# Attention, a dense layer and experts on one core: the dense layer's first activation queued inside attention, the sum of v taken from a column of constants, the embeddings on GpSimd

## The chip, the cores and the metric

The kernel runs on one core of one Trainium2 chip. The metric is the device time of one execution in microseconds (us); the time shown for a kernel is the median of its runs.

## The reference

Three parts follow each other. The sizes are 2 batches, 8 heads, 768 tokens of 64 values for attention, 1536 tokens of 512 values for the layers behind it, 2048 hidden values in the dense layer, and 8 experts of 1024.

```python
mask = q_bucket[:, :, :, None] == k_bucket[:, :, None, :]      # 6 sign bits of q @ proj, k @ proj
scores = np.where(mask, scale * np.matmul(q, k.transpose(0, 1, 3, 2)), -1e9)
attn = np.exp(scores - np.max(scores, axis=-1, keepdims=True))
attn = attn / (np.sum(attn, axis=-1, keepdims=True) + 1e-09)
x = np.matmul(attn, v)                                         # then to [1536, 512]
h = x @ w_in
x = (h * np.tanh(softplus(h))) @ w_out                         # dense layer
logits = normalized(x) @ normalized(expert_emb).T / tau        # each token goes to its best expert
out = gate * (np.maximum(x @ w1[e], 0.0) @ w2[e])              # e, gate: of that expert
```

## The kernel before, in words

**Attention** (class `Attn`). Heads are taken one after the other, each in six key tiles of 128 keys. `run_all` (L473) is a loop over steps g from -2 to 101. A step computes the scores of one key tile (`score_unit`, L360: four matmuls into PSUM, and one Exp on ScalarE into an SBUF tile p of 128 keys x 768 queries), one and a half max units for a head further on (`max_unit`, L316, reduced by VectorE at L328 and L332), and two products with v for the key tile three steps back (`pv`, L395: each is two instructions, since the operands are 32 bits wide). p tiles come from a pool of five buffers. Everything else has a place in the table `AT` (L37), in sixths of a step counted from the head's first: `out0` and `out1` copy the two halves of a finished head out of PSUM (ScalarE, L425, and L427 for the sums of an odd head), `s_row` to `xlo` divide by the sums and split the result into two halves of 16 bits.

The sum of v, times 1e-9/768, is added to the product before the division. `v_red` (L374) adds the tiles of v on GpSimd in six instructions a pair of heads, `v_sum` (L384) sums over the 128 partitions with a small matmul (two instructions), `v_col` (L390) copies the column from PSUM with ScalarE, and `scale` (L455) adds it. They are placed at 2 to 17, at 62 and at 66 sixths of a step, in every second head: eight times in all.

**PSUM in attention** has eight banks: two score tiles of two banks each (`ps_s`), two buffers of the pool `ps_m` and two of `ps_o` for the products. `ps_m` serves the max tiles, the column sp of v_sum, the row transposes tm (L348, first heads only), the embedding's transposes tpe (L752), and the first two hidden tiles of the dense layer.

**The hook** (L1283) runs after every step. It takes one step of `emb` (L723: the experts' embeddings are normalized, split and transposed; the three instructions L744 to L746 run after step 8 and the transposes after step 10), computes the hidden tile of block 0 after step 95 and of block 1 after step 99 (`UP`), and takes one step of `w1_work` (L671), which splits the dense weights: three VectorE instructions (L700, L702, L682), then two on ScalarE (L709, L710) and a subtraction on GpSimd (L711). Two steps of it are left at the end of attention; the last tile goes through L716 (ScalarE) and L718 (VectorE).

**The dense layer** (`moe1`, L775) has 48 blocks G of 128 hidden values x 512 tokens. The hidden tile h of a block is 12 matmuls (`up`, L760), its product with w_out another 12 (L815), three blocks later. The activation between them is, on ScalarE, Tanh (L834), Square (L839), Square (L845), Exp (L848) and, behind VectorE's L857, Square (L861); then, in the next block's turn, VectorE's L836 and L841, ScalarE's conversion L850 and GpSimd's subtraction L851. Block 0 has PE compute the hidden tiles 2 to 5; from block 3 on each block computes one more, three ahead. A hidden tile's buffer is free after L841. The activation has four tiles t, w, u and p with two buffers each; L857 writes p from w and u, and L841 writes p again.

**Order.** `in_order` (L126) ties each engine's instructions to the order in which the program issues them, so an engine's queue is the order of the code. The experts (`moe2`) follow.

Of the kernel before, what the change touches and what calls it, by code (L numbers as in the profile page):

```python
# [20 lines left out]
P = 128  # L21
# [6 lines left out]
PB = 5  # L28
# [5 lines left out]
TEND = 101  # L34
RPB, CVB = 1, 3
STEP = 7
AT = dict(rows_t=-7, rows_in=-7, m_row=-22, bits=-102, max_end=-24, hi=-184, lo0=-156, lo1=-150, dup=-138, out_x=-147, in_x=-127, out_m=-99, in_m=-79, args=-103, load_kq=-210, load_v=-37, v_red=2, v_sum=62, v_col=66, out0=50, out1=54, s_row=55, inv=77, r_out=79, r_in=91, scale=112, xhi=127, xlo=139)  # L37
GAP = dict(bits=1, max_end=1, inv=1, v_red=3)
STEPS = dict(v_red=6, bits=3, max_end=2, inv=2)
FROM = dict(rows_in=1, m_row=4, bits=3, max_end=1, hi=4, lo0=4, lo1=4, dup=4, out_x=4, in_x=4, out_m=4, in_m=4, rows_t=1, args=3, load_kq=6, load_v=2)  # L40
UNTIL = dict(rows_t=4, rows_in=4)
EVERY = dict(load_kq=(2, 0), load_v=(2, 0), v_red=(2, 0), v_sum=(2, 0), v_col=(2, 0)) | {k: (2, 1) for k in ("inv", "r_out", "r_in", "scale", "xhi", "xlo")}
# [95 lines left out]
class Attn:  # L138
    def __init__(self, tc, ctx, q, k, v, proj, ident, ones, xx, dt, rest):
# [40 lines left out]
        self.tiny = cp.tile([P, 1], F32, name="tiny")  # L180
        nc.gpsimd.memset(self.tiny, 1e-9 / S)
# [14 lines left out]
    def warm(self, n, w=None):  # L196

        if w is None:
            w = self.ps_o.tile([P, HS], F32, tag="o", name="warmed")
        for _ in range(n):  # L200
            self.nc.tensor.matmul(w, self.ones, self.ones[:, 0:1].to_broadcast([P, HS]), start=True, stop=True)
# [158 lines left out]
    def score_unit(self, b, h, t):  # L360
        nc = self.nc
        z = self.Z[b, h]
        kq, m = z["x"], z["m"]
        ts = self.tok(b, h, t)
        s = self.ps_s.tile([P, 2, 512], F32, tag="s", name=f"s_{b}_{h}_{t}")[:, :, 0:HS]
        for c in range(2):
            nc.tensor.matmul(s[:, c, :], kq[:, 0, ts], kq[:, 1, c * HS : (c + 1) * HS], start=True, stop=False)  # L367
        for c in range(2):
            nc.tensor.matmul(s[:, c, :], m[0:97, 0, ts], m[0:97, 1, c * HS : (c + 1) * HS], start=False, stop=True)  # L369
        p = self.pp.tile([P, S], F32, tag="p", name=f"p_{b}_{h}_{t}", bufs=PB)  # L370
        nc.scalar.activation(p.rearrange("p (c n) -> p c n", c=2), s, AF.Exp, scale=2.0**-11)  # L371
        z["p"].append(p)

    def v_red(self, b, h):  # L374
        add = partial(self.nc.gpsimd.tensor_tensor, op=ALU.add)
        vs = self.Z[b, h]["vs"] = self.sm.tile([P, 2, D], F32, tag="vs", name=f"vs_{b}_{h}", bufs=1)
        for i in range(2):
            v = self.vn(b, h + i)
            t = self.sm.tile([P, 3, D], F32, tag="vt", name=f"vt_{b}_{h + i}", bufs=1)
            yield add(t, v[:, 0:3], v[:, 3:6])  # L380
            yield add(t[:, 0], t[:, 0], t[:, 1])
            yield add(vs[:, i], t[:, 0], t[:, 2])

    def v_sum(self, b, h):  # L384

        z = self.Z[b, h]
        z["sp"] = self.ps_m.tile([P, 1], F32, tag="m", name=f"sp_{b}_{h}")
        self.nc.tensor.matmul(z["sp"], z.pop("vs").rearrange("p i d -> p (i d)"), self.tiny, start=True, stop=True)

    def v_col(self, b, h):  # L390
        z = self.Z[b, h]
        z["col"] = self.sm.tile([P, 1], F32, tag="col", name=f"col_{b}_{h}")
        self.nc.scalar.copy(z["col"], z.pop("sp"))

    def pv(self, b, h, t, c):  # L395

        nc = self.nc
        z = self.Z[b, h]
        i, cs = h % 2, slice(c * HS, (c + 1) * HS)
        m = P if i else 65  # L400
        if t == 0:
            z["o", c] = self.ps_o.tile([P, HS], F32, tag="o", name=f"o_{b}_{h}_{c}")
        o = z["o", c][0:m, :]
        nc.tensor.matmul(o, self.vn(b, h, t), z["p"][t][:, cs], start=(t == 0), stop=(t == NJ - 1))  # L404

    def wide(self, b, h, tag, bufs):

        last = b == B - 1 and h >= H - 2
        name = tag
        pool, tag, bufs = (self.rest_pools[0], "stg", None) if last else (self.ou, tag, bufs)  # L410
        return pool.tile([P, S], F32, tag=tag, name=f"{name}_{b}_{h}", bufs=bufs)

    def out(self, b, h, c):

        z = self.Z[b, h]
        i, cs = h % 2, slice(c * HS, (c + 1) * HS)
        o = z.pop(("o", c))
# [32 lines left out]
    def r_in(self, b, h):  # L450
        self.rb = self.wide(b, h, "rb", 1)
# [154 lines left out]
class Moe:  # L606
# [116 lines left out]
    def emb(self, tp, ps):  # L723
# [50 lines left out]

    def moe1(self, side, more):  # L775
# [22 lines left out]
        for G in range(N + GLAG):  # L798
            c, F = divmod(G, NF1)
            if G < N:  # L800
                t, w, u, p = m[G] = [T(tag, G) for tag in "twup"]
# [36 lines left out]
            if G < N:  # L838
                nc.scalar.activation(w, t, AF.Square, scale=-0.5, bias=self.bias[0.5])  # L839
# [14 lines left out]
            for x in new[:NC]:  # L854
                x(0)
            if G < N:
                nc.vector.scalar_tensor_tensor(p, w, 1.0, u, op0=ALU.add, op1=ALU.mult)  # L857
# [3 lines left out]
                nc.scalar.activation(t, p, AF.Square, bias=self.bias[-1.5])  # L861
# [395 lines left out]
def moe_attn(ctx, tc, a):  # L1257
# [9 lines left out]
    with ExitStack() as c1:  # L1267
# [7 lines left out]
        with ExitStack() as c2, tc.using_default_side("right"):  # L1275
# [88 lines left out]
```

## Time and profile before

| | |
|---|---|
| runs | 704.41 us median of 3 (703.2 to 705.53) |
| profiled execution | 708.11 us, of it a span of 706.3 us from the first to the last instruction |
| TensorE matmuls (PE) | 682.7 us busy, 97% of the span |
| VectorE (DVE) | 452.2 us, 64% |
| ScalarE (ACT) | 473.3 us, 67% |
| GpSimd (POOL) | 177.2 us, 25% |
| mean granted clock of TensorE | 0.988 of full |

In the profile's rows L12 stands for line 12 of the kernel. An instruction is named by its line, its engine, its operation and its tiles, out<-in. PEld is TensorE's loading of weights. Idle time before an instruction stands in brackets with what ended it. Attention lasts until about 265 us, the dense layer until about 530 us.

### The profile page before, as it was taken

How to read it: one execution, taken by the hardware profiler on the slowest of the kernel's cores; microseconds unless marked ns; L12 is line 12 of the kernel's file. 1: busy time of each engine (PE TensorE's matmuls, PEld its weight loads, DVE VectorE, ACT ScalarE, POOL GpSimd, SP SyncE). 2: the span in 40 equal slices, each digit the busy share in tenths (PEclk: the TensorE clock that was granted, in tenths of full speed). 3: DMA queues.
4: the chain of work that ended last, by engine and by line, in shares of the span. 5: the costliest groups of instructions: out<-in, count | busy, mean ns of one | idle time of the engine just before them, and what ended most of it. 6: DMA issues, size and time to landing. Idle time of an engine off the chain costs nothing. (4 is left out here: it accounts for less than half of the span.)

```text
span 706.3 us, 10526 instructions
## 1 busy us (share of the span) xinstructions
PE 682.7 (97%) x3896; PEld 382.8 (54%) x3896; DVE 452.2 (64%) x751; ACT 473.3 (67%) x722; POOL 177.2 (25%) x206
## 2 busy tenths in 40 slices
PE   7889999999999998999999999999999999999995
PEld 4445556565565553444444444444467766667772
DVE  8776798888977736766647554544556555565620
ACT  5656686776757659999859877887745555556530
POOL 3122233132231322322225352432421111101011
PEclk9999999999999999999999999999999999999998
DMA  5386998999976312444012010210255999888700
GB/s 158 105 216 179 206 262 225 210 255 212 202 176 178 93 52 85 134 134 127 23 65 50 9 60 1 83 38 1 84 193 179 258 300 279 261 243 239 196 23 20
DMA packets 127467, 102.67 MB, mean 145 GB/s; under 512 B 88231, under 2 KB 106663, under 8 KB 127410
## 3 DMA queue, kind: packets, MB, share of 16 engines
q1 hardware_dynamic: 112610, 81.18, 45.3%
q10 hardware_dynamic: 12560, 14.45, 6.1%
q0 software_dynamic: 2240, 6.31, 2.8%
q8 instruction: 32, 0.52, 0.3%
q14 instruction: 25, 0.20, 0.1%
HBM read 63.47 MB, written 24.21 MB: 124 GB/s over the span
## 5 line engine op out<-in xcount | busy, mean ns | idle before, releaser
L404 PE MATMUL o<-p,vn 128*65 128x384 f32 (+1 forms) x384 | 154.3, 488 | 0.4
L772 PE MATMUL h<-xx,wi 128*128 128x512 f16 x576 | 133.2, 382 | 2.1 <-DVE p L841 2.1
L815 PE MATMUL x<-wo,g 128*128 128x512 f16 x576 | 131.3, 379 | 0.0
L371 ACT ACTIVATE p<-s 128x768 f32<-128x768 f32 x96 | 77.3, 807 | 59.9 <-PE s L369 41.4
L851 POOL TENSOR_TENSOR g<-p,g 128x512 f16<-128x512 f32 x48 | 57.6, 1200 | 157.2 <-ACT g L850 136.6
L772 PEld LDWEIGHTS <-wi 128*128 128x128 f16 x576 | 56.5, 99 | 71.0 <-issue 5.3
L815 PEld LDWEIGHTS <-g 128*128 128x128 f16 x576 | 56.4, 98 | 68.0 <-POOL g L851 0.3
L1152 PE MATMUL y<-b,hh 128*128 128x512 f16 x384 | 84.2, 379 | 0.0
L1138 PEld LDWEIGHTS <-a 128*128 128x128 f16 x768 | 75.1, 98 | 10.9 <-issue 0.7
L404 PEld LDWEIGHTS o<-p,vn 128*65 128x65 f32 (+1 forms) x384 | 59.7, 165 | 29.2 <-issue 13.2
L1138 PE MATMUL h<-xt,a 128*128 128x256 f16 x672 | 74.7, 273 | 0.4 <-DMA xt<-xs 0.4
L857 DVE SCALAR_TENSOR_TENSOR p<-w,u 128x512 f32<-128x512 f32 x48 | 33.2, 692 | 63.0 <-ACT u L848 63.0
L328 DVE TENSOR_REDUCE mx<-ms 128x1 f32<-128x512 f32 x96 | 65.3, 687 | 12.8 <-PE ms L327 11.2
L1152 PEld LDWEIGHTS <-hh 128*128 128x128 f16 x384 | 37.6, 98 | 43.6
L1157 POOL DMA_INDIRECT out_dram<-o,row x16 | 16.2, 1012 | 151.8 <-ACT o L1156 135.6
L836 DVE SCALAR_TENSOR_TENSOR t<-t,u 128x512 f32<-128x512 f32 x48 | 39.7, 827 | 22.5 <-ACT t L861 22.5
L653 DVE SCALAR_TENSOR_TENSOR b<-st,b 128x1024 f16<-128x1024 f32 x28 | 33.1, 1222 | 24.9 <-ACT b L652 24.9
L653 DVE SCALAR_TENSOR_TENSOR a<-st,a 128x1024 f16<-128x1024 f32 x28 | 34.3, 1224 | 22.0 <-ACT a L652 22.0
L367 PE MATMUL s<-tx 128*128 128x384 f16 x192 | 48.0, 332 | 0.0
L332 DVE TENSOR_REDUCE mx<-ms 128x2 f32<-128x512 f32 x48 | 33.0, 687 | 23.3 <-PE ms L331 23.2
L369 PE MATMUL s<-tm 97*128 97x384 f16 x192 | 47.7, 330 | 0.0
L1144 ACT ACTIVATE hh<-h 128x512 f16<-128x512 f32 x32 | 19.1, 596 | 35.9 <-PE h L1138 34.8
(181 smaller groups left out, 967.5 us busy)
## 6 DMA issues: line engine op xcount, KB each, us to landing
st<-in_moe_w_dram SPq DMA_DIRECT2D x32, 1024.0 KB, 5.8
stg<-in_moe_w_in_dram SPq DMA_DIRECT2D x16, 512.0 KB, 4.8
stg<-in_moe_w_out_dram SPq DMA_DIRECT2D x16, 512.0 KB, 4.3
dx<-ka ACTq DMA_DIRECT2D x12, 384.0 KB, 5.3
dm<-kq ACTq DMA_DIRECT2D x12, 384.0 KB, 3.0
xs<-zrow SPq DMA_DIRECT2D x16, 257.0 KB, 7.4
vn<-in_v_dram SPq DMA_DIRECT2D x16, 192.0 KB, 5.9
rb<-rd SPq DMA_DIRECT2D x16, 192.0 KB, 4.3
```

What stands on the lines that cost most here:

```text
L328: nc.vector.tensor_reduce(z["mx"][:, j, 0:1], s, axis=AX.X, op=ALU.max)
L367: nc.tensor.matmul(s[:, c, :], kq[:, 0, ts], kq[:, 1, c * HS : (c + 1) * HS], start=True, stop=False)
L369: nc.tensor.matmul(s[:, c, :], m[0:97, 0, ts], m[0:97, 1, c * HS : (c + 1) * HS], start=False, stop=True)
L371: nc.scalar.activation(p.rearrange("p (c n) -> p c n", c=2), s, AF.Exp, scale=2.0**-11)
L404: nc.tensor.matmul(o, self.vn(b, h, t), z["p"][t][:, cs], start=(t == 0), stop=(t == NJ - 1))
L653: nc.vector.scalar_tensor_tensor(lo, src, sc, hi, op0=ALU.mult, op1=ALU.subtract)
L772: self.nc.tensor.matmul(h, self.wi[wu][:, k, fs], x[:, k, xs], start=(i == 0), stop=(i == 3 * NKT - 1))
L815: nc.tensor.matmul(x2[r], gf[:, gu, rs], self.wo[wu][:, f, :], start=(f == 0 and gu + wu == 0), stop=(f == NF1 - 1 and gu == 1))
L836: nc.vector.scalar_tensor_tensor(t1, t1, 0.75, u1, op0=ALU.add, op1=ALU.mult)
L851: nc.gpsimd.tensor_tensor(g[G - 1][:, 1, :], p1, g[G - 1][:, 0, :], op=ALU.subtract)
L1138: nc.tensor.matmul(h[:, v, :], W[0][wu][:, k, fs], xt[e][:, xu * NKT + k, :], start=(i == 0), stop=(i == 3 * NKT - 1))
L1152: nc.tensor.matmul(y[s], hs[F // 2][:, hu, F % 2, s * P : (s + 1) * P], W[1][wu][:, F, :], start=(F == 0 and hu + wu == 0), stop=(F == NF2 ...
```

## The change

- The p tiles are five fixed tiles of 769 columns; the last column is set to 1e-9/768 once. The second half of each product with v takes this column along, so the sum of v comes out as column 768 of the copied tile w, and `scale` reads it there. `v_red`, `v_sum` and `v_col` are gone, with their places in `AT`.
- Two of the p tiles (1 and 2) lie side by side in a tile of a pool that lives on in the dense layer. Block 0's activation uses them as its three tiles: `pre` issues Tanh and Square after step 96, Square and Exp after step 97, VectorE's product and the last Square after step 98. `moe1` issues nothing of this for block 0.
- The activation has three tiles: L857's result is written over w, and L841's too.
- The embedding's three instructions move from VectorE to GpSimd, and its transposes one step back.

```diff
+PRE = {96: 2, 97: 2, 98: 2}
-AT = dict(..., load_v=-37, v_red=2, v_sum=62, v_col=66, out0=50, ...)
+AT = dict(..., load_v=-37, out0=50, ...)
...
-        self.tiny = cp.tile([P, 1], F32, name="tiny")
-        nc.gpsimd.memset(self.tiny, 1e-9 / S)
+        self.PT, self.pt = [], 0
+        self.two = rest[1].tile([P, 2 * (S + 1)], F32, name="p12")
+        for i in range(PB):
+            if i in (1, 2):
+                p = self.two[:, (i - 1) * (S + 1) : i * (S + 1)]
+            else:
+                p = self.pp.tile([P, S + 1], F32, name=f"p{i}", bufs=1)
+            nc.gpsimd.memset(p[:, S : S + 1], 1e-9 / S)
+            self.PT.append(p)
...
-        p = self.pp.tile([P, S], F32, tag="p", name=f"p_{b}_{h}_{t}", bufs=PB)
-        nc.scalar.activation(p.rearrange("p (c n) -> p c n", c=2), s, AF.Exp, scale=2.0**-11)
+        p = self.PT[self.pt % PB]
+        self.pt += 1
+        nc.scalar.activation(p[:, 0:S].rearrange("p (c n) -> p c n", c=2), s, AF.Exp, scale=2.0**-11)
...
-        i, cs = h % 2, slice(c * HS, (c + 1) * HS)
+        i, cs = h % 2, slice(c * HS, (c + 1) * HS + c)
...
-        o = z["o", c][0:m, :]
+        o = z["o", c][0:m, 0 : HS + c]
...
-        self.nc.scalar.copy(z["w"][r, cs], o[r, :])
+        self.nc.scalar.copy(z["w"][r, cx], o[r, 0 : HS + c])
...
-        self.nc.vector.scalar_tensor_tensor(self.rb, self.Z[b, h]["w"], self.Z[b, h - 1]["col"], self.rb, op0=ALU.add, op1=ALU.mult)
+        w = self.Z[b, h]["w"]
+        self.nc.vector.scalar_tensor_tensor(self.rb, w[:, 0:S], w[:, S : S + 1], self.rb, op0=ALU.add, op1=ALU.mult)
...
-        nc.vector.tensor_scalar(e32, e32, ss, 256.0, op0=ALU.mult, op1=ALU.mult)
-        nc.vector.tensor_copy(en[:, 0, :], e32)
-        nc.vector.tensor_tensor(en[:, 1, :], e32, en[:, 0, :], op=ALU.subtract)
+        nc.gpsimd.tensor_scalar(e32, e32, ss, 256.0, op0=ALU.mult, op1=ALU.mult)
+        nc.gpsimd.tensor_copy(en[:, 0, :], e32)
+        nc.gpsimd.tensor_tensor(en[:, 1, :], e32, en[:, 0, :], op=ALU.subtract)
+        yield
         yield
         yield
...
+    def pre(self, buf):
+
+        nc = self.nc
+        t, w, u = (buf[:, i * CH : (i + 1) * CH] for i in range(3))
+        self.m0 = t, w, u
+        yield nc.scalar.activation(t, self.h[0], AF.Tanh, scale=2.0**-13)
+        yield nc.scalar.activation(w, t, AF.Square, scale=-0.5, bias=self.bias[0.5])
+        yield nc.scalar.activation(u, w, AF.Square, scale=C1, bias=self.bias[C2])
+        yield nc.scalar.activation(u, u, AF.Exp, bias=self.bias[C3])
+        yield nc.vector.scalar_tensor_tensor(w, w, 1.0, u, op0=ALU.add, op1=ALU.mult)
+        yield nc.scalar.activation(t, w, AF.Square, bias=self.bias[-1.5])
...
-            if G < N:
-                t, w, u, p = m[G] = [T(tag, G) for tag in "twup"]
+            if G == 0:
+                m[0] = self.m0
+            elif G < N:
+                t, w, u = m[G] = [T(tag, G) for tag in "twu"]
+            new_g = 0 < G < N
...
-                t1, _, u1, p1 = m.pop(G - 1)
+                t1, p1, u1 = m.pop(G - 1)
...
-            if G < N:
+            if new_g:
                 nc.scalar.activation(t, h[G], AF.Tanh, scale=2.0**-13)
...
+            if new_g:
+                nc.vector.scalar_tensor_tensor(w, w, 1.0, u, op0=ALU.add, op1=ALU.mult)
...
+            pre = moe.pre(at.two)
...
                 for f in behind:
                     f()
+                for _ in range(PRE.get(g, 0)):
+                    next(pre, None)
```

## Rows read from the trace of the kernel before

**Rows 1.** Who TensorE's matmuls waited for: us in total, times, longest us.
```profile
PE h L772 <- DVE p L841: 2.1, 1, 2.1
PE ms L327 <- DVE mx L328: 2.0, 6, 0.8
```

**Rows 2.** Stretches: us, each engine's busy time (instructions), granted clock, DMA share, GB/s.
```profile
14.00:16.00 2.00, 1.82 (x24) 1.43 (x25) 1.46 (x3) 0.65 (x2) 1.30 (x2) 1.00 0.03 8
...
54.00:56.00 2.00, 1.78 (x13) 1.25 (x13) 0.02 (x1) 0.33 (x3) 0.00 (x0) 0.53 0.56 143
...
282.00:284.00 2.00, 1.35 (x4) 0.55 (x4) 0.69 (x2) 1.94 (x4) 0.00 (x0) 0.71 0.89 189
```

**Rows 3.** Timeline of TensorE, 44 to 60 us: start, duration, instruction, idle before.
```profile
44.50 0.49 PE L367 MATMUL s<-tx 128*128 128x384 f16 x2
...
49.05 0.49 PE L367 MATMUL s<-tx 128*128 128x384 f16 x2
...
50.56 0.28 PE L388 MATMUL sp<-tiny,vs 128*128 128x1 f32 x2
51.69 0.38 PE L327 MATMUL ms<-tm 96*128 96x512 f16 x1 [0.85 <-DVE mx L328]
...
52.85 0.49 PE L348 MATMUL tm<-ident,m 128*1 128x128 f16 x6
54.22 0.35 PE L752 MATMUL tpe<-ident,en 8*128 8x8 f16 x8 [0.88 <-ACT tm L352]
...
58.15 0.49 PE L367 MATMUL s<-tx 128*128 128x384 f16 x2
```

**Rows 4.** Timeline of all engines, 256 to 300 us.
```profile
258.40 2.75 PE L772 MATMUL h<-xx,wi 128*128 128x512 f16 x12
...
264.42 0.47 ACT L425 COPY ou<-o 64x384 f32<-64x384 f32 x1 [5.06 <-PE o L404]
...
268.23 0.58 ACT L834 ACTIVATE t<-h 128x512 f32<-128x512 f32 x1
268.40 1.28 POOL L711 TENSOR_TENSOR wo<-cv,wo 128x512 f16<-128x512 f32 x1 [7.80 <-ACT cv L710]
268.69 1.53 DVE L682 SCALAR_TENSOR_TENSOR cv<-stg,cv 128x512 uint32<-128x512 uint32 x1
...
270.97 0.61 ACT L716 ACTIVATE wo<-cv 128x512 f16<-128x512 f32 x1
...
271.83 0.72 ACT L861 ACTIVATE t<-p,bias 128x512 f32<-128x512 f32 x1 [0.24 <-DVE p L857]
272.45 0.58 ACT L834 ACTIVATE t<-h 128x512 f32<-128x512 f32 x1
...
282.65 4.44 PE L772 MATMUL h<-xx,wi 128*128 128x512 f16 x12 [2.09 <-DVE p L841]
```

**Rows 5.** Timeline of TensorE behind the v_sum pair of 84 us.
```profile
84.47 0.38 PE L327 MATMUL ms<-tm 96*128 96x512 f16 x1 [0.17 <-DVE mx L328]
```

**Rows 6.** The costliest groups, the products: count | busy us, mean ns | idle before.
```profile
L404 PE MATMUL o<-p,vn 128*65 128x384 f32 (+1 forms) x384 | 154.3, 488 | 0.4
```

**Rows 7.** Timeline of VectorE near 47 us.
```profile
47.39 0.47 DVE L744 TENSOR_SCALAR e<-e,ess 8x512 f32<-8x512 f32 x1
```

**Rows 8.** Timeline of GpSimd, 0 to 75 us.
```profile
38.92 0.31 POOL L382 TENSOR_TENSOR vs<-vt 128x64 f32<-128x64 f32 x1 [8.86 <-issue]
```

**Rows 9.** Timeline, 256 to 300 us: GpSimd's read of block 0, ScalarE's second step of block 2.
```profile
275.88 1.16 POOL L851 TENSOR_TENSOR g<-p,g 128x512 f16<-128x512 f32 x1 [6.20 <-ACT g L850]
...
277.29 0.72 ACT L839 ACTIVATE w<-t,bias 128x512 f32<-128x512 f32 x1
```

**Rows 10.** The instructions of line 682: count, duration in ns min/median/max, starts, forms.
```profile
L682 DVE SCALAR_TENSOR_TENSOR cv<-stg,cv x32: 665/682/1534, 44.7 to 268.7; 128x512 uint32<-128x512 uint32 x32
```

**Rows 11.** Timeline of TensorE, 10 to 30 us.
```profile
14.18 0.31 PE L288 MATMUL ar<-pj,tx 128*128 128x18 f16 x6 [1.12 <-ACT tx L222]
```

**Rows 12.** ScalarE's groups by line: count | busy us, mean ns | idle before, releaser.
```profile
L834 ACT ACTIVATE t<-h 128x512 f32<-128x512 f32 x48 | 28.1, 586 | 18.2 <-PE h L772 18.2
```

More of the change, by code (lines that the diff above doesn't have):

```diff
@@ L34 @@
 TEND = 101
+PRE = {96: 2, 97: 2, 98: 2}
 RPB, CVB = 1, 3
 STEP = 7
-AT = dict(rows_t=-7, rows_in=-7, m_row=-22, bits=-102, max_end=-24, hi=-184, lo0=-156, lo1=-150, dup=-138, out_x=-147, in_x=-127, out_m=-99, in_m=-79, args=-103, load_kq=-210, load_v=-37, v_red=2, v_sum=62, v_col=66, out0=50, out1=54, s_row=55, inv=77, r_out=79, r_in=91, scale=112, xhi=127, xlo=139)
-GAP = dict(bits=1, max_end=1, inv=1, v_red=3)
-STEPS = dict(v_red=6, bits=3, max_end=2, inv=2)
+AT = dict(rows_t=-7, rows_in=-7, m_row=-22, bits=-102, max_end=-24, hi=-184, lo0=-156, lo1=-150, dup=-138, out_x=-147, in_x=-127, out_m=-99, in_m=-79, args=-103, load_kq=-210, load_v=-37, out0=50, out1=54, s_row=55, inv=77, r_out=79, r_in=91, scale=112, xhi=127, xlo=139)
+GAP = dict(bits=1, max_end=1, inv=1)
+STEPS = dict(bits=3, max_end=2, inv=2)
 FROM = dict(rows_in=1, m_row=4, bits=3, max_end=1, hi=4, lo0=4, lo1=4, dup=4, out_x=4, in_x=4, out_m=4, in_m=4, rows_t=1, args=3, load_kq=6, load_v=2)
 UNTIL = dict(rows_t=4, rows_in=4)
-EVERY = dict(load_kq=(2, 0), load_v=(2, 0), v_red=(2, 0), v_sum=(2, 0), v_col=(2, 0)) | {k: (2, 1) for k in ("inv", "r_out", "r_in", "scale", "xhi", "xlo")}
+EVERY = dict(load_kq=(2, 0), load_v=(2, 0)) | {k: (2, 1) for k in ("inv", "r_out", "r_in", "scale", "xhi", "xlo")}
 LAST = ("inv", "r_out", "r_in", "scale", "xhi", "xlo")
@@ L198, in warm @@
         if w is None:
-            w = self.ps_o.tile([P, HS], F32, tag="o", name="warmed")
+            w = self.ps_o.tile([P, HS + 1], F32, tag="o", name="warmed")[:, 0:HS]
         for _ in range(n):
@@ L369, in score_unit @@
             nc.tensor.matmul(s[:, c, :], m[0:97, 0, ts], m[0:97, 1, c * HS : (c + 1) * HS], start=False, stop=True)
-        p = self.pp.tile([P, S], F32, tag="p", name=f"p_{b}_{h}_{t}", bufs=PB)
-        nc.scalar.activation(p.rearrange("p (c n) -> p c n", c=2), s, AF.Exp, scale=2.0**-11)
+        p = self.PT[self.pt % PB]
+        self.pt += 1
+        nc.scalar.activation(p[:, 0:S].rearrange("p (c n) -> p c n", c=2), s, AF.Exp, scale=2.0**-11)
         z["p"].append(p)
[L374 to L393, printed above, removed]
     def pv(self, b, h, t, c):
@@ L398, in pv @@
         z = self.Z[b, h]
-        i, cs = h % 2, slice(c * HS, (c + 1) * HS)
+        i, cs = h % 2, slice(c * HS, (c + 1) * HS + c)
         m = P if i else 65
         if t == 0:
-            z["o", c] = self.ps_o.tile([P, HS], F32, tag="o", name=f"o_{b}_{h}_{c}")
-        o = z["o", c][0:m, :]
+            z["o", c] = self.ps_o.tile([P, HS + 1], F32, tag="o", name=f"o_{b}_{h}_{c}")
+        o = z["o", c][0:m, 0 : HS + c]
         nc.tensor.matmul(o, self.vn(b, h, t), z["p"][t][:, cs], start=(t == 0), stop=(t == NJ - 1))
@@ L410, in wide @@
         pool, tag, bufs = (self.rest_pools[0], "stg", None) if last else (self.ou, tag, bufs)
-        return pool.tile([P, S], F32, tag=tag, name=f"{name}_{b}_{h}", bufs=bufs)
+        return pool.tile([P, S + 1], F32, tag=tag, name=f"{name}_{b}_{h}", bufs=bufs)
     def out(self, b, h, c):
@@ L416, in out @@
         i, cs = h % 2, slice(c * HS, (c + 1) * HS)
+        cx = slice(c * HS, (c + 1) * HS + c)
         o = z.pop(("o", c))
@@ L422, in out @@
                 z["w"] = self.Z[b, h - 1]["w"]
-            z["s"] = self.wide(b, h, "su", 1)[0:1, :] if i else z["w"][64:65, :]
+            z["s"] = self.wide(b, h, "su", 1)[0:1, :] if i else z["w"][64:65, 0:S]
         r = slice(D, P) if i else slice(0, 65)
-        self.nc.scalar.copy(z["w"][r, cs], o[r, :])
+        self.nc.scalar.copy(z["w"][r, cx], o[r, 0 : HS + c])
         if i:
-            self.nc.scalar.copy(z["s"][:, cs], o[0:1, :])
+            self.nc.scalar.copy(z["s"][:, cs], o[0:1, 0:HS])
     def out0(self, b, h):
@@ L439, in s_row @@
         row = self.Z[b, h].pop("s")
-        self.nc.sync.dma_start(self.rs[:, h % 2, :], row.rearrange("o (p j) -> o p j", j=NJ))
+        self.nc.sync.dma_start(self.rs[:, h % 2, :], row[:, 0:S].rearrange("o (p j) -> o p j", j=NJ))
     def inv(self, b, h):
@@ L450, in r_in @@
     def r_in(self, b, h):
-        self.rb = self.wide(b, h, "rb", 1)
+        self.rb = self.wide(b, h, "rb", 1)[:, 0:S]
         for i in range(2):
@@ L843, in moe1 @@
                 x(1)
-            if G < N:
+            if new_g:
                 nc.scalar.activation(u, w, AF.Square, scale=C1, bias=self.bias[C2])
             fill(FILL[1])
-            if G < N:
+            if new_g:
                 nc.scalar.activation(u, u, AF.Exp, bias=self.bias[C3])
@@ L860, in moe1 @@
                 fill(FILL[2])
-                nc.scalar.activation(t, p, AF.Square, bias=self.bias[-1.5])
+            if new_g:
+                nc.scalar.activation(t, w, AF.Square, bias=self.bias[-1.5])
             while late:
```

3 lines of the change are left out of this document (1 added, 2 removed).

## Prediction

> **What bounds the kernel now.** I read the profile in this order: busy time by engine, then who TensorE waited for, then its granted clock by stretches, then the timelines of the stretches that stood out. TensorE (PE) is busy nearly throughout (table above), so time can be won only where PE idles, runs at the low clock, or does work that the change takes away. PE's waits name the places [rows 1]: one of 2.1 us of the dense layer's matmuls for VectorE (DVE), and six of the max matmuls for DVE's reductions, 2.0 us together, the longest 0.8. After two of these places the granted clock falls towards half, the lower of its two levels (1.2 and 2.4 GHz): it reads 0.53 in 54 to 56 us and 0.71 in 282 to 284 us, where PE had been late just before [rows 2].
>
> The first place is steps 10 and 11 of attention [rows 3]. The two steps before take 49.05 - 44.50 = 4.55 us; these two take 9.10 us, until 58.15, though they hold the same scores, maxima and products, and beside them only three small things: the v_sum pair (0.28), the row transposes tm (0.49) and the embedding's transposes tpe (0.35). The reason is the pool of two PSUM buffers that max tiles, sp, tm and tpe share: sp holds one until ScalarE (ACT) copies it four positions later, so everything between goes through the other, one at a time behind its reader. PE waits 0.85 us before a max matmul and 0.88 before tpe.
>
> The second place is the start of the dense layer [rows 4]. ACT idles 5.06 us before the copies of the last head (264.42), though the first hidden tile is ready earlier: its 12 matmuls start at 258.40 and take 2.75 us. Its Tanh runs only at 268.23, the next tile's at 272.45: a block takes 4.22 us of chained ACT and DVE work. PE has filled all hidden buffers by then and waits until 282.65 for DVE's product L841, 2.09 us, and then takes 4.44 us for 12 matmuls instead of 2.75.
>
> **The sum of v** (v_red, v_sum, v_col). Removed: 48 GpSimd additions, eight pairs of small matmuls, eight ACT copies, eight holds of a PSUM buffer. At the first of the eight, the two steps should take 4.55 + 0.49 + 0.35 = 5.4 us in place of 9.10, because tm and tpe then find a second buffer and the clock has no reason to fall: 3.7 us. The embedding's extra yield moves tpe to the end of step 11 and its reader to the end of step 12, so that it now holds a buffer over a step with two max matmuls. I take 0.3 us for that, between the 0.17 and 0.85 that PE waits at such a hold [rows 3, 5], nearer to the 0.17, since DVE has less to do there after the change. So 3.4 us; the ends are 1.1 (the pair and the one wait; the rest comes back as other waits) and 3.9 (no time left between the matmuls). At the other seven the pair takes 0.28 of PE, and at four of them (84, 114, 144, 173 us) PE waits another 0.17, as at the first of them [rows 5]: 7 x 0.28 + 4 x 0.17 = 2.6 us, between 0.7 (only the waits) and 2.7. Added: one column in half of the products, 154.3 us / 384 / 2 = 0.2 us [rows 6], and four more small initialisations on GpSimd at the start, beside the first loads. Two of the five p tiles lie side by side, so that one begins 769 words behind the other; no row shows what such a start costs a moving operand. The weights of the odd heads begin 65 words into their tile already, and their products lie in one group with the others [rows 6]; I take nothing.
>
> **Embeddings on GpSimd.** Three instructions leave DVE, from 47.39 [rows 7]. On GpSimd each lies between 0.31 us (64 elements [rows 8]) and 1.16 (512 elements, two inputs [rows 9]), 0.9 to 3.5 together, so they end at 48.3 to 50.9. tpe wants them at the end of step 11, 49.05 + 4.9 = 54 us, so at least 3 us cover them and the price is nothing. Behind them in GpSimd's queue one subtraction of a weight's low half waits, about 1 us at most; it is read only in the dense layer.
>
> **The first activation inside attention.** Tanh, two Squares and Exp are queued at steps 96 and 97; behind the waiting Tanh stand only the last head's copies, which are not ready before 264.42 anyway. Tanh can start when the first hidden tile is complete, 258.40 + 2.75 = 261.15, and the four take what they took, 2.74 us from Tanh to the instruction behind them (268.23 to 270.97 [rows 4]): 263.9, just inside ACT's idle time. DVE, idle there, has its product ready before the first pair of copies ends. The last Square is queued between the two pairs; it takes 0.62 us from its start to the next instruction's (271.83 to 272.45), and delays all behind it on ACT by that: the second pair, a cast of xx, the two conversions of a weight.
>
> What is late next? Not block 1's Tanh by its input, but by order: before it ACT converts the last weight tile (L716), which waits for DVE's L682. L682 ran from 268.69 for 1.53 us, until 270.22. It stands behind ACT's cast by way of two DVE instructions, and beside a GpSimd subtraction (268.40, 1.28 us) that stands behind ACT's conversions; so the whole group slides by 0.62. L682 ends at 270.84, L716 (0.61) at 271.45, and block 1's Tanh starts there instead of at 272.45. The chain wins 1.0 us, not the 4.2 of a block, and PE's wait shrinks from 2.09 to 1.1 us.
>
> Is L682 held in this way? It reads two SBUF tensors and has a median of 0.68 us, with 1.53 as the longest of 32 [rows 10], and the longest runs beside the subtraction. The Trainium skill, GPSIMD Engine Reference (section Key points), says that GpSimd shares its SBUF interfaces with VectorE and contends with VectorE's instructions that have two SBUF inputs; by that rule the hold stays, and the trace agrees, with 1.53 against 0.68. If the hold fell away, L716 would be free 0.85 us sooner, PE's wait would be 0.25, and the transition would give 3.5 us.
>
> Does the clock stay up after 1.1 us? At 14.18 PE had been idle for 1.12 us [rows 11], and the granted clock of 14 to 16 us is 1.00 [rows 2]. I take that it stays, which gives 4.44 - 2.75 = 1.7 us. The transition gives 1.0 + 1.7 = 2.7; the ends are 1.0 (low clock) and 3.8 (no wait).
>
> **Three tiles instead of four.** The product is written over w, so ACT's second step of block G+2 now waits for GpSimd's read of block G. That read ended at 275.88 + 1.16 = 277.04 and the step ran at 277.29 [rows 9]: 0.25 us to spare, no cost.
>
> **Sum.** 3.4 + 2.6 - 0.2 + 2.7 = 8.5 us. PE's wait for L841 comes once [rows 1], so what PE wins at the transition arrives at the end. The profiled execution took 708.11 us (span 706.3), 3.7 above the median of the runs: 708.11 - 8.5 = 699.6, and by the same difference 704.41 - 8.5 = **695.9 us**.
>
> **Rivals.**
> (1) The clock falls after 1.1 us as it did after 2.09: 1.7 less, 697.6. For it: 0.85 and 0.88 us near each other were enough at 54 us [rows 2, 3]. Against it: 14.18. Chance 0.18.
> (2) The change doesn't do what it says in attention: DVE ends the same waits without sp. That keeps 1.1 + 0.7 there, 4.3 in all with the 0.2 and the 2.7: 700.1. For it: DVE ends most of PE's waits [rows 1]. Against it: behind the pair at 84 us PE waits only 0.17. Chance 0.12.
> (3) L682 isn't held: 9.3, 695.1; with no wait left and 3.9 at the first place, 10.2, 694.2. Chance 0.05.
> (4) GpSimd's first scalar instruction of this kind has to fetch its code. GpSimd stood still for 8.86 us, with nothing in the profile to wait for, after the broadcast of tau [rows 8]. A second such pause from 47.39 would end at 56.3 and the three instructions at up to 59.8, while PE wants them at 54: 5.8 us of idle PE and 1.7 of low clock leave 1.0 us: 703.4, no change. The Trainium skill, GPSIMD Engine Reference (section Instruction dispatch), says that the first call to a freshly loaded kernel pays a load that shows as no instruction; the trace agrees with the 8.86 us, but its ordinary elementwise instructions start without one. Chance 0.06.
> (5) Slower: ACT's wait for GpSimd at the second step (L839) decides the dense layer. A block takes ACT 4.22 us and PE up to 5.5 (24 matmuls, 12 in 2.75), so GpSimd's read must end more than 0.25 + 1.3 us later than now before PE feels it; from there each 0.1 us costs 0.1 in each of some 45 blocks. At 1.9 us later: 0.35 x 45 = 15.8 against the 8.5 won, 711.7. For it: GpSimd has other work in some blocks. Against it: ACT waits 18.2 us in all for PE's hidden tiles [rows 12], so it gets ahead of PE and a single late read is made up. Chance 0.07, with other losses of that sign.
>
> **Numbers.** The forecast as worked out has 0.52. A measurement can tell about 0.3% here, 2.1 us. Faster: 0.52 + 0.18 + 0.12 + 0.05 = 0.87; same 0.06; slower 0.07. The range goes from (3) at its best, 694.2, less 1.2 for the scatter of the runs, to (2) with 0.3: 693.0 to 700.4. (4) and (5) are left out.
>
> **What would show it.** Right: no wait of 0.85 us at step 10, the clock at 1.00 through steps 10 and 11, and 5.4 to 5.9 us for the two; Tanh of block 0 as soon as its 12 matmuls end; L716 still the last thing before block 1's Tanh; one PE wait of about 1.1 us before the seventh hidden tile, and 2.75 us for its 12 matmuls. Wrong: tpe waiting for GpSimd, PE waiting for DVE at the old places of sp, ACT waiting for GpSimd in the dense layer, or a second stretch of low clock at the transition.

## The result, and the profile after

The changed kernel takes **699.15 us** (median of 5 runs, 697.6 to 699.89) where the kernel before takes 705.53 in the runs beside it: a ratio of **0.9896**, 95% interval 0.9861 to 0.9931. Timed once more it was 0.9896 again (0.9863 to 0.9928). The forecast of 695.9 against 704.41 is a ratio of 0.9879. The time lies inside the forecast range; the gain of the medians, 6.4 us, is a quarter below the forecast 8.5, which the interval of the ratio (4.9 to 9.8 us) still holds.

The profiled execution took 699.19 us, its span is 697.4 against 706.3. PE is the first thing to read again, by the same view of who it waited for (us in total, times, longest us):

```profile
PE ms L335 <- DVE mx L340: 1.5, 3, 0.6
PE tm L356 <- DVE mx L336: 1.3, 1, 1.3
PE h L763 <- DVE w L847: 1.0, 1, 1.0
...
PE ms L335 <- DVE mx L336: 0.5, 1, 0.5
```

The wait for L841 was 2.1 us [rows 1] and is 1.0 (its line is L847 now). The max matmuls' six waits of 2.0 us for the first reduction (L328, now L336) are one of 0.5. That one (at 24.73 us) and the three of 1.5 us for the other reduction are in the kernel before too. But there is a line that was not there: the row transposes tm wait 1.3 us for the first reduction. PE's timeline at steps 10 and 11, to be read against [rows 3], with one row of VectorE (L746, which reads tpe):

```profile
48.33 0.49 PE L375 MATMUL s<-tx 128*128 128x384 f16 x2
...
52.22 0.49 PE L356 MATMUL tm<-ident,m 128*1 128x128 f16 x6 [1.35 <-DVE mx L336]
...
54.92 0.35 PE L743 MATMUL tpe<-ident,en 8*128 8x8 f16 x8
55.20 0.50 PE L375 MATMUL s<-tx 128*128 128x384 f16 x2
55.54 0.49 PE L377 MATMUL s<-tm 97*128 97x384 f16 x2
55.87 0.38 PE L335 MATMUL ms<-tm 96*128 96x512 f16 x1
56.09 0.81 PE L392 MATMUL o<-p,vn 128*128 128x384 f32 x2
57.03 0.38 PE L335 MATMUL ms<-tm 96*128 96x512 f16 x1
57.25 0.81 PE L392 MATMUL o<-p,vn 128*128 128x385 f32 x2
58.05 0.18 DVE L746 COPY enT<-tpe 128x64 f16<-128x64 f16 x1
58.19 0.69 PE L296 MATMUL ar<-pj,tx 128*128 128x18 f16 x12
```

The two steps take 55.20 - 48.33 = 6.87 us instead of 9.10. In the step behind them two instructions start 0.29 us late each: 57.03 stands 0.94 behind 56.09, where 0.65 is usual, and 58.19 as much behind 57.25. Both lie before L746 has read tpe, or at its end, so that only one of the two buffers is free for them. The transition to the dense layer, with the same starts as in [rows 4] (all engines):

```profile
252.71 2.75 PE L763 MATMUL h<-xx,wi 128*128 128x512 f16 x12
255.49 0.60 ACT L771 ACTIVATE p<-h 128x512 f32<-128x512 f32 x1 [1.84 <-PE h L763]
...
263.62 1.53 DVE L672 SCALAR_TENSOR_TENSOR cv<-stg,cv 128x512 uint32<-128x512 uint32 x1
...
265.19 0.63 ACT L706 ACTIVATE wo<-cv 128x512 f16<-128x512 f32 x1 [1.94 <-DVE cv L672]
265.72 0.58 ACT L840 ACTIVATE t<-h 128x512 f32<-128x512 f32 x1
...
275.85 2.75 PE L763 MATMUL h<-xx,wi 128*128 128x512 f16 x12 [0.98 <-DVE w L847]
278.44 2.75 PE L821 MATMUL x<-wo,g 128*128 128x512 f16 x12
```

Tanh of block 0 (L771) runs as soon as its matmuls end. Block 1's (L840) waits for the last weight tile (L706), which waits for a DVE instruction held for 1.53 us. PE's wait is 0.98 us and its 12 matmuls take 2.75. From the first hidden tile to the second group of products it is 25.74 us instead of 28.53 (286.93 in the kernel before).

The gain by stages, in profiled executions (us; the transition runs to the second group of products):

| stage | before | after | gain |
|---|---|---|---|
| start to step 10 | 49.05 | 48.33 | 0.72 |
| steps 10 and 11 | 9.10 | 6.87 | 2.23 |
| step 12 to the first hidden tile | 200.25 | 197.50 | 2.75 |
| transition | 28.53 | 25.74 | 2.79 |
| from there to the last matmul | 411.23 | 410.81 | 0.42 |

The first and the last of these gains are not the change's. The last, 0.42 us, is nearly all one wait for a DMA among the experts, which the profile of the kernel before has and the changed kernel's has not:

```profile
552.88 9.88 PE L1138 MATMUL h<-xt,a 128*128 128x256 f16 x89 [0.36 <-DMA xt<-xs]
```

The first is no larger than scatter: the changed kernel, profiled again (e11 below), starts step 10 at 49.04 us, like the kernel before. In the runs below this start lies anywhere from 46.95 to 50.94 us, as the granted clock of the first 40 us differs. The last stage takes 409.1 us where the mean clock of 500 to 560 us is 1.00 (e5, e10, e12), 410.7 to 411.2 where it is 0.97, as in both kernels here, and 412.1 to 412.3 where it is 0.94 (e1, e4, e7). So kernels are compared below by the three stages in the middle, 7.77 us here, and by time only where several rounds were run.

### The profile page after: what moved, and what is told of

Same layout as the page of the kernel before. It is cut to its first block, busy times and chain, and to the rows that moved or that the text cites. A ratio compares the mean times of both kernels' runs of the same rounds, so it can differ in the third digit from the quotient of the medians.

```text
span 697.4 us, 10447 instructions
## 1 busy us (share of the span) xinstructions
PE 676.5 (97%) x3880; PEld 379.1 (54%) x3880; DVE 449.6 (64%) x748; ACT 472.2 (68%) x714; POOL 154.7 (22%) x165
## 5 line engine op out<-in xcount | busy, mean ns | idle before, releaser
L392 PE MATMUL o<-p,vn 128*65 128x384 f32 (+3 forms) x384 | 153.3, 486 | 0.2
L763 PE MATMUL h<-xx,wi 128*128 128x512 f16 x576 | 131.5, 379 | 1.1 <-DVE w L847 1.0
L857 POOL TENSOR_TENSOR g<-w,g 128x512 f16<-128x512 f32 x47 | 55.4, 1178 | 150.5 <-ACT g L856 107.9
L336 DVE TENSOR_REDUCE mx<-ms 128x1 f32<-128x512 f32 x96 | 65.4, 688 | 10.3 <-PE ms L335 8.5
L863 DVE SCALAR_TENSOR_TENSOR w<-w,u 128x512 f32<-128x512 f32 x47 | 32.5, 692 | 61.2 <-ACT u L854 59.0
```

Of the source, the lines that this page charges most:

```text
L336: nc.vector.tensor_reduce(z["mx"][:, j, 0:1], s, axis=AX.X, op=ALU.max)
L763: self.nc.tensor.matmul(h, self.wi[wu][:, k, fs], x[:, k, xs], start=(i == 0), stop=(i == 3 * NKT - 1))
L857: nc.gpsimd.tensor_tensor(g[G - 1][:, 1, :], p1, g[G - 1][:, 0, :], op=ALU.subtract)
```

## The experiments

**What holds tm at step 10.** The theory: GpSimd's new instructions hold VectorE, and with it the maxima. The timeline of both engines in the changed kernel:

```profile
48.28 1.15 POOL L736 TENSOR_TENSOR en<-e,en 8x512 f16<-8x512 f32 x1
48.49 2.61 DVE L692 SCALAR_TENSOR_TENSOR cv<-stg,cv 128x512 uint32<-128x512 uint32 x1
49.40 1.15 POOL L701 TENSOR_TENSOR wi<-cv,wi 128x512 f16<-128x512 f32 x1
...
51.49 1.28 DVE L336 TENSOR_REDUCE mx<-ms 128x1 f32<-128x512 f32 x2
```

L692 has a median of 0.68 us and takes 2.61 here. It starts while the embedding's last instruction runs, and ends 0.55 us after the weight's subtraction behind that. Two runs take the three instructions away from there.

```diff
 e1_emb_dve
-        nc.gpsimd.tensor_scalar(e32, e32, ss, 256.0, op0=ALU.mult, op1=ALU.mult)
-        nc.gpsimd.tensor_copy(en[:, 0, :], e32)
-        nc.gpsimd.tensor_tensor(en[:, 1, :], e32, en[:, 0, :], op=ALU.subtract)
+        nc.vector.tensor_scalar(e32, e32, ss, 256.0, op0=ALU.mult, op1=ALU.mult)
+        nc.vector.tensor_copy(en[:, 0, :], e32)
+        nc.vector.tensor_tensor(en[:, 1, :], e32, en[:, 0, :], op=ALU.subtract)
 e2_emb_early
-        for _ in range(6):
+        for _ in range(3):
...
         nc.gpsimd.tensor_tensor(en[:, 1, :], e32, en[:, 0, :], op=ALU.subtract)
+        for _ in range(3):
+            yield
```

> The changed kernel with the three embedding instructions back on VectorE. In the changed kernel VectorE's L692 lasts 2.61 us at 48.49, beside GpSimd's L736 and L701, and TensorE waits 1.35 us before tm; steps 10 and 11 take 6.87 us (48.33 to 55.20). Theory (GpSimd's embedding instruction holds L692): L692 falls to about 0.7 us, VectorE carries 1.6 us more, the wait before tm shrinks to 0.7 to 1.1, the two steps take 6.2 to 6.7 us. Rival (VectorE is simply full there): with 1.6 us more on it the wait grows, the two steps take 7.0 to 8.4 us.

> The changed kernel with the embedding's normalization and its three GpSimd instructions three steps earlier (after step 5), the transposes where they are. Theory (the collision of GpSimd's L736 with VectorE's L692 makes tm late): L692 below 1.7 us (only the weight's subtraction L701 can still hold it), the wait before tm below 0.6, steps 10 and 11 in 5.7 to 6.2 us in place of 6.87. Rival (tm waits for its buffer whatever GpSimd does): the two steps stay at 6.7 to 7.0 us.

With the instructions back on VectorE, steps 10 and 11 take 5.62 us (46.95 to 52.57); three steps earlier on GpSimd, 5.47 (50.78 to 56.25). Both are shorter than the theory gave (6.2 to 6.7 and 5.7 to 6.2). In the first:

```profile
47.80 0.67 DVE L692 SCALAR_TENSOR_TENSOR cv<-stg,cv 128x512 uint32<-128x512 uint32 x1
...
49.59 0.49 PE L356 MATMUL tm<-ident,m 128*1 128x128 f16 x6
```

The hold and the wait are gone together. The contention costs 1.25 to 1.40 us, all of tm's wait. In the second the instructions meet another L692 (43.99 us, 1.55 long), behind which PE doesn't wait. The times, 698.0 and 699.6 in one run each, say little: the second one's step 10 starts 2.45 us later than the changed kernel's.

Which of the two is held isn't always the same. In the kernel before, L702 (now L692) and the subtraction start almost together:

```profile
49.86 2.19 POOL L711 TENSOR_TENSOR wi<-cv,wi 128x512 f16<-128x512 f32 x1 [8.55 <-ACT cv L710]
49.90 0.67 DVE L702 SCALAR_TENSOR_TENSOR cv<-stg,cv 128x512 uint32<-128x512 uint32 x1
50.49 0.54 DVE L262 SCALAR_TENSOR_TENSOR ka<-kq,ka 128x384 f16<-128x384 f32 x1
```

There VectorE's two instructions take their usual time and the subtraction 2.19 us in place of 1.15; e1 has the same (0.67 and 2.19). In the changed kernel GpSimd was already at work when L692 started.

**What the sum of v had cost.** Three runs put back one piece of it each, with unused results: the pair, the hold and the copy (e7); only the pair, written into an open max tile (e8, seven times); only GpSimd's additions (e10).

```diff
 e7_sp
-AT = dict(..., xlo=139)
+AT = dict(..., xlo=139, v_sum=62, v_col=66)
...
+        z["sp"] = self.ps_m.tile([P, 1], F32, tag="m", name=f"sp_{b}_{h}")
+        self.nc.tensor.matmul(z["sp"], self.vs, self.tiny, start=True, stop=True)
...
+        self.nc.scalar.copy(col, z.pop("sp"))
 e8_pair
+            if h % 2 == 1 and b * H + h >= 3 and j == 3:
+                nc.tensor.matmul(s[:, 0:1], self.vs, self.tiny, start=True, stop=True)
 e10_adds
-GAP = dict(bits=1, max_end=1, inv=1)
-STEPS = dict(bits=3, max_end=2, inv=2)
+GAP = dict(bits=1, max_end=1, inv=1, v_red=3)
+STEPS = dict(v_red=6, bits=3, max_end=2, inv=2)
...
+            yield add(t, v[:, 0:3], v[:, 3:6])
+            yield add(t[:, 0], t[:, 0], t[:, 1])
+            yield add(vs[:, i], t[:, 0], t[:, 2])
```

> The changed kernel with a pair of small matmuls, its hold of a PSUM buffer and ScalarE's copy put back at the eight old places, on a constant operand and without GpSimd's additions; its result is not used. If these three are what the sum of v cost, steps 10 and 11 grow again by at least 0.9 us, to 7.8 to 9.1, and the stretch from step 12 to the first hidden tile grows by 2.4 to 2.9 us, from 197.5 to about 200.2. Rival: GpSimd's additions, which contend with VectorE, were part of the cost; then the stretch grows by less than 1.7 us.

> The changed kernel with only the pair of small matmuls put back, written into the max tile that is open anyway, so that no buffer is held and ScalarE copies nothing; seven pairs, one in every second head from the fourth on; the result is not used. If PE's time for the pair is most of the cost, the stretch from step 12 to the first hidden tile grows by 6 or 7 times 0.28, 1.7 to 2.0 us, to 199.2 to 199.5, and the kernel with the hold is only 0.7 to 1.0 us longer there. Rival: the hold is most of it; then this one grows by less than 1 us. Steps 10 and 11 stay at 6.9 us, or up to 7.2 if a pair falls into them.

> The changed kernel with only GpSimd's 48 additions of v put back at their old places; nobody reads their sums. In the kernel before, the products behind a head's end waited four times for ScalarE's copies of the sums, 1.1 us together (97 and 127 us among them), and there VectorE's conversion of the signs had taken 0.51 us beside an addition in place of 0.20. If the additions caused this by way of VectorE, the four delays of 0.25 to 0.3 us come back and the stretch from step 12 to the first hidden tile grows by 1.0 to 1.2 us, from 197.5 to about 198.6. Rival: they came from the pair or from ScalarE's copy; then the stretch stays within 0.3 us of 197.5.

| | steps 10, 11 | step 12 to first hidden tile | time, one run |
|---|---|---|---|
| after | 6.87 | 197.50 | 699.15 (5 runs) |
| e7, pair + hold + copy | 8.03 | 199.64 | 705.59 |
| e8, pair alone | 6.88 | 199.28 | 700.92 |
| e10, additions alone | 9.16 | 198.34 | 702.11 |

Steps 10 and 11 grow by 1.16 us in e7, as expected. In the stretch behind them its steps with a pair are longer by 0.44 us (four of them), 0.29 (two) and 0.22 (one): 2.57 us. The table has only 2.14 because the changed kernel's own profile is late in two other steps, by 0.31 us in step 39 and 0.16 in step 66. e1, e2 and e3, whose edits leave this stretch alone, have neither and take 197.02 to 197.04 in it. Against these e7 grows by 2.6, inside the 2.4 to 2.9 expected.

e8 looks nearly as dear as e7 and isn't. One of its steps is 1.45 us longer for a DMA (tm, a wait of 1.27 us at 120.66), which has nothing to do with a pair: e11, without any, waits 0.37 us for the same DMA. The six steps with a pair are longer by 0.13 to 0.14 us each. Its row shows why:

```profile
49.17 0.28 PE L338 MATMUL ms<-tiny,vs 128*128 128x1 f32 x2
49.31 0.38 PE L341 MATMUL ms<-tm 96*128 96x512 f16 x1
```

The pair is listed with 0.28 us, but the next matmul starts 0.14 behind it. So a pair costs 0.14 and its hold up to 0.30 more. Six pairs make 0.81 us, less than the 1 us that the rival gave as its bound: the hold is most of the cost.

e10 shows a cost that the prediction had at zero, so the rival named with e7 had the right idea, though its bound of 1.7 us was not met. PE's weight loads in the kernel before wait for ScalarE's copy of the sums at the end of five heads between 96 and 215 us (the expectation counts four). The first is this one, and behind it the one of e10 at the same place, each with the VectorE instruction ahead of it in the same head:

```profile
92.44 0.60 POOL L380 TENSOR_TENSOR vt<-vn 128x192 f32<-128x192 f32 x1
92.59 0.51 DVE L299 TENSOR_SCALAR kq<-ag 128x72 f16<-128x72 f32 x1
...
96.73 0.19 PEld L404 LDWEIGHTS o<-p,vn 128*65 128x65 f32 x2 [0.34 <-ACT su L427]
```

```profile
93.82 0.60 POOL L389 TENSOR_TENSOR vt<-vn 128x192 f32<-128x192 f32 x1
93.97 0.51 DVE L307 TENSOR_SCALAR kq<-ag 128x72 f16<-128x72 f32 x1
...
98.11 0.19 PEld L402 LDWEIGHTS o<-p,vn 128*65 128x65 f32 x2 [0.33 <-ACT su L426]
```

The conversion takes 0.51 us beside an addition and 0.20 in the changed kernel. That makes the head's maxima late, then the DMA issue that waits for them on ScalarE, then the copies behind it in ScalarE's queue, then the buffer for the next products: 0.24 to 0.27 us each time. In e10 all five waits are back, at the places of the kernel before, and its stretch is 1.30 us longer than that of e1, e2 and e3. Against the changed kernel it is only 0.84, as one such wait (0.38 us at 123.14, step 39) is in the changed kernel's profile too, there behind a conversion of 0.20. That conversion starts late instead: VectorE's queue had stood still before it for a DMA (in e3, where L446 doesn't wait, the conversion is on time):

```profile
116.33 1.02 DVE L446 SCALAR_TENSOR_TENSOR rb<-ou,rb 128x768 f32<-128x768 f32 x1 [0.70 <-DMA rb<-rd]
```

The 0.16 us of step 66 stay unexplained. At steps 10 and 11 the additions queue up behind the embedding and the subtraction, and L692's counterpart is held still longer:

```profile
50.15 1.15 POOL L746 TENSOR_TENSOR en<-e,en 8x512 f16<-8x512 f32 x1
50.36 3.15 DVE L702 SCALAR_TENSOR_TENSOR cv<-stg,cv 128x512 uint32<-128x512 uint32 x1
51.26 1.15 POOL L711 TENSOR_TENSOR wi<-cv,wi 128x512 f16<-128x512 f32 x1
52.38 0.58 POOL L389 TENSOR_TENSOR vt<-vn 128x192 f32<-128x192 f32 x1
...
54.76 0.75 PE L356 MATMUL tm<-ident,m 128*1 128x128 f16 x6 [2.01 <-DVE mx L336]
```

So PE waits 0.66 us longer than in the changed kernel; the rest of the 2.29 us that steps 10 and 11 grow by comes with the clock, which falls here (last section). Beside three GpSimd instructions back to back the VectorE instruction takes 3.15 us, beside two 2.61, beside one 1.55 (e2): it ends 0.55 us after the last of them each time. The Trainium skill, SBUF — State Buffer (section SBUF: two separate sides), says that a VectorE instruction with two SBUF inputs and a GpSimd instruction that reads SBUF take a shared pair of ports as an exclusive lock: whichever starts first has it for the whole instruction, and the other is blocked. The trace agrees that the later one is blocked, with 2.61 us against 0.68; where the two started 0.04 us apart, it was GpSimd's (above). It shows more: the waiting VectorE instruction doesn't get its turn between two GpSimd instructions that follow each other without a gap, as far as GpSimd's spans, which are rough, can tell.

**The first activation.** One run issues its instructions only after attention's last step; one begins the split of the weights a little earlier, so that the last tile's L706 doesn't wait for DVE.

```diff
 e3_no_pre
-PRE = {96: 2, 97: 2, 98: 2}
+PRE = {}
...
+                for _ in pre:
+                    pass
 e4_w1_early
-CVS = ((4, 99, 1),)
+CVS = ((4, 99, 1), (90, 92, 1))
```

> The changed kernel with all six instructions of block 0's activation issued after attention's end, before the dense layer's first block; the rest of the change stays. Theory (the queue place of block 0 is what the transition won): TensorE waits 1.9 to 2.5 us before the seventh hidden tile, its 12 matmuls take about 4.4 us at the lower clock, the span is 2.5 to 3.3 us longer than the changed kernel's 697.4. Rival (the transition came from the three tiles or the memory's layout): wait near 1.0, 12 matmuls in 2.75, span within 0.7 us of 697.4.

> The changed kernel with two more steps of the weight splitting at steps 90 and 91, so that none is left for the dense layer and L706 no longer stands before block 1's Tanh. Theory (L706, waiting for L672, sets when block 1 starts): Tanh of block 1 begins 1.2 us or more earlier against the first hidden tile, TensorE's wait before the seventh hidden tile (0.98) is gone, the span is 0.7 to 1.1 us shorter. Rival (block 1 starts late for another reason, its hidden tile or the copies): the wait stays above 0.6.

e3, over 3 rounds, has a ratio of 0.9953 to the kernel before (0.9929 to 0.9978). Its transition takes 251.22 to 279.24, 28.02 us, 2.28 more than the changed kernel's. Against the expectation the clock has no part in that in the profiled execution: PE waits twice, and its matmuls keep 2.75 us for 12.

```profile
272.71 2.10 PE L821 MATMUL x<-wo,g 128*128 128x512 f16 x9 [1.16 <-DVE w L847]
276.65 2.75 PE L763 MATMUL h<-xx,wi 128*128 128x512 f16 x12 [1.83 <-DVE w L847]
```

But that execution, 700.52 us, is the shortest of e3's ten. Four of them have a mean granted clock of 0.993 (700.5 to 701.8 us), six one of 0.986 to 0.990 (702.5 to 704.8). Whether these six lose the clock at the transition, as expected, no profile shows; 28.02 us is the price without that.

e4's transition takes 24.59 us, 1.15 less than the changed kernel's; the wait before the seventh hidden tile is gone and L840 starts 11.2 us after the first hidden tile instead of 13.0. So the weight's split, not the activation, stood last there, as the prediction had it. But one product then waits for ScalarE in attention (0.29 us, "PE o <- ACT ou L414"), with 0.55 us lost in that step, which e5, e9 and e12 share. Its time was 700.26 us in one run.

**Three tiles alone**, in the kernel before:

```diff
 e6_three
-                t, w, u, p = m[G] = [T(tag, G) for tag in "twup"]
+                t, w, u = m[G] = [T(tag, G) for tag in "twu"]
...
-                nc.vector.scalar_tensor_tensor(p, w, 1.0, u, op0=ALU.add, op1=ALU.mult)
+                nc.vector.scalar_tensor_tensor(w, w, 1.0, u, op0=ALU.add, op1=ALU.mult)
```

> The kernel before with the activation's three tiles in place of four and nothing else. If the fourth tile was never needed, the dense layer keeps its times: 28.5 us from the first hidden tile to the second group of products, and 270 us or less from there to the experts as before; span and time within 0.4% of the kernel before. Rival: ScalarE's second step waits for GpSimd's read of two blocks ago; then the profile shows that wait on ScalarE, several us in all, and the dense layer is longer by the part of it that TensorE feels.

The transition takes 28.59 us (28.53 before), from there to the last matmul 410.75 (411.23), the whole 709.61 in one run beside a median of 707.91. In the list of waits ScalarE waits for GpSimd nowhere. Giving up the fourth tile cost nothing that these stages show.

**Both leaks closed.** Two versions, from the edits above: e2's with e4's (e5), and e1's with e4's (e9, and again as e12). e11 is the changed kernel, unedited, beside e12.

> The changed kernel with the embedding's three GpSimd instructions three steps earlier and the split of the dense weights begun earlier in steps 90 and 91. If the remaining loss at steps 10 and 11 (6.87 us against 5.47 with the instructions earlier) and at the transition (25.74 against 24.59 us) are both on the path and independent, the two gains add: steps 10 and 11 take 5.4 to 5.7 us, the transition 24.4 to 24.8, and the time is 2.5 us below the changed kernel's, 696.7, a ratio of 0.986 to the kernel before. Rival: a faster start of the dense layer is given back by a later wait of the dense layer on ScalarE or DMA; then the transition is shorter, the stretch behind it longer by the same 1.1 us, and the time is 697.8.

> The changed kernel with the embedding's three instructions back on VectorE and the same earlier split of the dense weights. If GpSimd's contention was the whole loss at steps 10 and 11, it does as well as the kernel with the instructions three steps earlier: steps 10 and 11 take 5.5 to 5.7 us, the transition 24.4 to 24.8, the time lies within 0.5 us of that kernel's, 696.7. Rival: VectorE's 1.5 us more before step 10 makes its max reductions late, PE waits there and the time is 697.5 or more.

> The changed kernel once more, beside the kernel with the embedding on VectorE and the weights' split begun earlier, so that the two are timed on one chip. 0.989 to 0.991 of the kernel before.

> The changed kernel with the embedding's three instructions on VectorE and the weights' split begun in steps 90 and 91, timed again. By stages it wins 1.24 us at steps 10 and 11 and 1.15 at the transition and loses 0.07 between them against the changed kernel's profile: 2.3 us less than the changed kernel on this chip, a ratio of 0.986 to the kernel before. Rival: the gains do not reach the end, and the two medians lie within 0.7 us.

| 5 rounds each | median us | ratio to before | 95% |
|---|---|---|---|
| after | 699.15 | 0.9896 | 0.9861 to 0.9931 |
| e11, after again | 699.92 | 0.9896 | 0.9863 to 0.9928 |
| e5 | 698.34 | 0.9871 | 0.9850 to 0.9891 |
| e9 | 697.72 | 0.9858 | 0.9836 to 0.9880 |
| e12, as e9 | 698.72 | 0.9875 | 0.9848 to 0.9903 |

By stages the gains add as expected: steps 10 and 11 take 5.47 us in e5 and 5.62 in e9 and e12, the transition 24.59 in all three, and the stretch between them 197.57 or 197.58. Against e11 on the same chip (6.88, 197.57, 25.73) e12 is 2.40 us shorter. That the stretch is as long as the changed kernel's is chance, though: e4's edit costs 0.55 us in it, and both profiles of the changed kernel are late there by about as much (0.47, and 0.54 in e11). With the 197.03 of e1 to e3 in e11's place, e12 is shorter by 1.9. PE's waits in e12 have neither tm nor the hidden tile left:

```profile
PE ms L335 <- DVE mx L340: 1.5, 3, 0.6
...
PE ms L335 <- DVE mx L336: 0.5, 1, 0.5
PE ms L335 <- ACT tm L230: 0.4, 1, 0.4
PE o L392 <- ACT ou L414: 0.3, 1, 0.3
```

By time e12 is 1.2 us below e11, between what the theory and the rival gave; e5 and e9, at 698.34 and 697.72, came out above their 696.7; and the intervals of all five overlap. All three medians of the two versions lie below both of the changed kernel; that they are faster at the end by the 1.9 to 2.4 us of the stages is not shown.

## Why the prediction was right, and where it was wrong

**The transition** was right in its mechanism and its size: forecast 2.7 us, measured 2.79. Every link held: Tanh at the end of the 12 matmuls, the slide of 0.62, L682 (now L672) held for 1.53 us as in [rows 10], L716 (L706) the last thing before block 1's Tanh, a wait of 0.98 against 1.1, the clock at 1.00. e3 confirms where it comes from, 2.28 us of it.

**The first place** is the step that failed. The forecast was 5.4 us for the two steps, 0.3 for the hold by tpe, a gain of 3.4. Without the embedding's contention they take 5.47 to 5.62, so what the freed buffer gives was right. The failed step is the one on the embeddings: "at least 3 us cover them and the price is nothing". It asked only when their result is wanted, and of the instruction behind them in GpSimd's queue only who reads it. It didn't ask whom they hold while they run. The rule needed was in the prediction itself, applied to L682 alone; the moved instructions run up to L692, which also reads two SBUF tensors. Measured price: 1.25 to 1.40 us. The hold by tpe is also dearer than the 0.3 taken: step 12 takes 3.53 us against 2.93, 0.60, as it delays two instructions and not one. That is read from the rows alone; no run puts the transposes back. It falls outside the two steps, so the place as a whole gave 2.23 - 0.60 = 1.63 us in place of 3.4.

**The other seven** were forecast at 2.6 us, and e7's steps give 2.57. The size was right and its split was not: the pair costs 0.14 and not 0.28, the hold up to 0.30 and not 0.17. The additions, which the prediction removed without a price, cost another 1.30 in e10, five waits. With 0.60 off for tpe the stretch should win 2.57 + 1.30 - 0.60 = 3.27; it won 3.2 where the two late steps are missing (e1, e2, e3) and 2.75 in the changed kernel's profile. The extra column, 0.2 us by the prediction, would be 0.02 over nine steps; over the nine from step 13 on the changed kernel is 0.01 us longer, which fits.

**Sum.** Forecast 8.5, in the three stages 7.77. That the total came out near is in part luck: two errors from one cause nearly met, as GpSimd's contention was overlooked where it was added (1.25 to 1.40) and where it was removed (1.30, of which 0.84 shows in the changed kernel's profile).

**Rivals.** (1) didn't happen: the clock stayed at 1.00 at the transition. (2) was half right: a wait took the place of another, but behind a held VectorE and not its ordinary maxima. (3) didn't happen either, L672 was held. (4) didn't: GpSimd's new scalar instruction (L734, 0.78 us) starts without a pause behind the instruction that it needs. (5) didn't: the changed kernel's dense layer keeps its time, and so does e6's.

## What to carry to other kernels

An instruction moved to GpSimd is priced twice: by when its result is wanted, and by which VectorE instructions run beside it. Look for the largest durations of VectorE's two-input lines (median against maximum in the view of one line): each outlier names a neighbour on GpSimd, and a removed GpSimd instruction can give time back in the same way. The cost of a small matmul is read from the start of the next one, not from its own duration. And one profile has waits of its own: here 0.47 us in a stretch of 197, seen only beside runs whose edits leave that stretch alone.

## What the runs showed of the hardware

Idle time alone didn't tell when the clock falls. In e7 PE idled 2.10 us before a max matmul (53.10) and the granted clock stayed; in e10 it idled 2.01 us at the same step and the clock fell to half. The stretches from 52 to 58 us, first of e7, then of e10 (us, each engine's busy time, granted clock, DMA share, GB/s):

```profile
52.00:54.00 2.00, 0.90 (x3) 0.38 (x2) 1.53 (x3) 0.00 (x0) 0.00 (x0) 1.00 0.10 20
54.00:56.00 2.00, 1.87 (x14) 1.14 (x13) 1.27 (x3) 1.18 (x3) 0.00 (x0) 1.00 0.05 11
56.00:58.00 2.00, 2.00 (x18) 1.15 (x17) 1.02 (x2) 1.21 (x2) 0.00 (x0) 1.00 0.89 232
```

```profile
52.00:54.00 2.00, 0.75 (x3) 0.21 (x2) 2.00 (x2) 0.00 (x0) 1.61 (x3) 1.00 0.63 140
54.00:56.00 2.00, 1.24 (x8) 0.74 (x8) 2.00 (x5) 0.46 (x1) 0.00 (x0) 0.71 0.00 0
56.00:58.00 2.00, 2.00 (x6) 0.98 (x5) 0.37 (x1) 1.40 (x3) 0.00 (x0) 0.50 0.38 79
```

In e3 waits of 1.16 and 1.83 us, with 2.1 us of matmuls between them, left it at 1.00 as well, where the kernel before lost it after 2.09 [rows 2, 4]. What else decides stays open here.

The other surprise is that a GpSimd instruction over 8 partitions (L736, 1.15 us) runs as long as one over 128 of the same 512 columns (L701, 1.15 us).
